# One row-tile pair for the lone rows of wo, other column groups for the last tile, and a new order of all work

## The chip, the cores and the metric

The kernel runs on one NeuronCore of a Trainium2 chip. The metric is device time in microseconds (us), the median over several executions. The core has TensorE (PE; its weight loads are shown as PEld), VectorE (DVE), ScalarE (ACT), GpSimd (POOL), and SyncE (SP), which here only issues DMAs. Matmuls read on-chip memory and write eight accumulator banks of 512 float32 columns (banks 0 to 7); DVE and ACT empty them.

## What is computed

x is 2048 tokens of 448 features. Two branches work on its layernorm and are added to it: linear attention with softmax feature maps of q and k (16 heads of 28), and an MLP mixer with token shifts.

```python
def _A_ref(x, wqkv, w_phi, wo):
    qkv = (x @ wqkv).reshape(B, S, 3, H, Dh).transpose(2, 0, 3, 1, 4)
    q, k, v = qkv[0], qkv[1], qkv[2]
    pq = einsum("bhsd,hdf->bhsf", q, w_phi); pk = einsum("bhsd,hdf->bhsf", k, w_phi)
    phi_q = concat([softmax(pq), softmax(-pq)]); phi_k = concat([softmax(pk), softmax(-pk)])
    kv = einsum("bhsf,bhsd->bhfd", phi_k, v); z = einsum("bhsf->bhf", phi_k)
    num = einsum("bhqf,bhfd->bhqd", phi_q, kv)
    den = einsum("bhqf,bhf->bhq", phi_q, z)[..., None] + 1e-6
    return (num / den).transpose(0, 2, 1, 3).reshape(B, S, D) @ wo

def _B_ref(x, w1, w2, w3, w4):
    h = gelu(layernorm(x) @ w1)
    # the four quarters of h's features are shifted by 1, -1, 2, -2 tokens
    x1 = x + concat([g0, g1, g2, g3]) @ w2
    return x1 + gelu(layernorm(x1) @ w3) @ w4

xn = layernorm(x)
out = x + _A_ref(xn, ...) + _B_ref(xn, ...)
```

## The kernel before

**An order written by hand.** Every operation is first recorded (`Recorder`, lines 20 to 222), each engine's stream in the order of recording. `solve()` (76) works out who must wait for whom; an engine waits only for semaphores, so the recording order is the order on each engine's queue, SP's and POOL's among them, and what two engines do at one time follows from the waits. Lines 118 to 120 hold PE's own rule: a matmul on a bank waits for earlier PE work on that bank if that came from another row tile (`lo != tile[0]`). All matmuls are recorded at line 204, all transposes on PE at 208, ACT's activations at 212, DVE's and POOL's operations at 216, DMA transposes at 219 and plain DMAs at 222, so the profile's lines are these helpers' and the tiles' names tell steps apart (some share memory: oT and o_tok lie in xnT's region, xs and outb in vaug's, h3T in phik's, eq in hi's, wo in wv's).

**Row tiles.** 448 rows are cut into four overlapping pieces of 128 that begin at 0, 128, 192 and 320 (`START`, 448). Nearly all matmuls use 64 rows, one on the array's lower half (`LO`) and one on its upper half (`HI`) at the same time. Rows 192 to 256 stand in two pieces, so in piece 1 or piece 2 one half is left out: seven steps of 64 rows make 448.

**The stages.** (1) `spin` and `hold` matmuls on constants keep PE busy until data is there. (2) `chain` (573 to 637, called at 969) lays out the first layernorm, transposes of xn (`XT`: on PE; `XD`: by DMA), v (`ZV`), w1 (`ZW`, `ZH`, `ZR`), the folding of w_phi into the q and k weights (`FO`), shifts of h (`h_shift`, six DMAs) and the start of the first token pair (`HF`: p = 0 k, 1 w2, 2 q; second number: first or second half). `L` holds layernorm steps: m statistics, r the root on POOL, q the root on ACT, a the apply on DVE, p on POOL. (3) `play` (1055) holds the rest as a list of steps: for token pairs k and q projections with exponentials (`k0`, `k1`, `q0`, `q1`), `w0`/`w1_` (w2 and its addition on DVE), `kn` (sums of phi_k on DVE), `kx` (their product on POOL), `K` (phi_k times v), `lo`/`sc`/`A` (second layernorm: statistics on DVE, scaling on POOL, apply on POOL or, for tiles in `on_dve`, on DVE), `G` and `T` (DMA transposes of its result and of exp(q)), `kc`/`kb` (the finished kv), `a`/`b` (w3 and its gelu), `N` (numerators: 16 matmuls, six DVE and two POOL operations, then a DMA transpose o_T), `f, 1..4, p` (for two tiles w4 and wo summed in banks 4 and 5, then `fin_out` on DVE) and `S` (the store).

**The end.** Tiles 14 and 15 come alone, after the list, with 128-row matmuls: `fin_full(14)` does 14 steps of w4 and four of wo at 448 columns; `fin_split(15, 256)` does the same for columns 0 to 256 and then 256 to 448, each followed by its addition and its store. Since four full pieces of wo would count rows 192 to 256 twice, `num_tile` (807 to 811) sets 64 columns of o_tok to zero for these two tiles.

Of the kernel before, what the change touches and what calls it, by code (L numbers as in the profile page):

```python
# [1111 lines left out]
```

## Time and profile before

| | us |
|---|---|
| median of three executions | 173.25 |
| lowest and highest | 173.14, 176.32 |
| the profiled execution | 172.24 |
| its span, first to last instruction | 170.5 |
| granted TensorE clock | 1.00 |

| engine | busy us | share |
|---|---|---|
| PE | 166.2 | 97% |
| DVE | 108.4 | 64% |
| POOL | 92.2 | 54% |
| ACT | 83.9 | 49% |

Times in the profile count from the span's start. A matmul's busy time is longer than its share of the array, because matmuls are pipelined; the distance from one start to the next tells what it costs. In the windows of the profile, after the length come busy us and number of instructions of PE, PEld, DVE, ACT and POOL, then the granted clock, the DMA engines' share and GB/s. In a timeline a bracket gives the idle time ahead of a group and who ended it.

### The profile page before, as it was taken

How to read it: one execution, taken by the hardware profiler on the slowest of the kernel's cores; microseconds unless marked ns; L12 is line 12 of the kernel's file. 1: busy time of each engine (PE TensorE's matmuls, PEld its weight loads, DVE VectorE, ACT ScalarE, POOL GpSimd, SP SyncE). 2: the span in 40 equal slices, each digit the busy share in tenths (PEclk: the TensorE clock that was granted, in tenths of full speed). 3: DMA queues.
4: the chain of work that ended last, by engine and by line, in shares of the span. 5: the costliest groups of instructions: out<-in, count | busy, mean ns of one | idle time of the engine just before them, and what ended most of it. 6: DMA issues, size and time to landing. Idle time of an engine off the chain costs nothing.

```text
span 170.5 us, 5420 instructions
## 1 busy us (share of the span) xinstructions
PE 166.2 (97%) x2351; PEld 96.3 (56%) x2351; DVE 108.4 (64%) x246; ACT 83.9 (49%) x114; POOL 92.2 (54%) x128
## 2 busy tenths in 40 slices
PE   8899999999999999999999999999999999999994
PEld 7576789655555555554554554554545555545463
DVE  3798865249999799967678933757407552425621
ACT  5789866879999879357242240421304222404000
POOL 6588590005799999992585272094420754023740
PEclk9999999999999999999999999999999999999999
DMA  5995677999599940569037949945440113021141
GB/s 153 359 207 99 150 84 210 190 351 171 118 134 191 257 98 0 142 126 94 0 64 136 113 96 168 139 105 78 92 115 0 35 31 112 4 58 31 31 117 48
DMA packets 51111, 20.07 MB, mean 118 GB/s; under 512 B 42256, under 2 KB 50384, under 8 KB 51088
## 3 DMA queue, kind: packets, MB, share of 16 engines
q1 hardware_dynamic: 49968, 18.86, 58.1%
q10 hardware_dynamic: 1120, 0.87, 1.5%
q8 instruction: 18, 0.29, 0.8%
q14 instruction: 5, 0.04, 0.1%
HBM read 7.14 MB, written 1.84 MB: 53 GB/s over the span
## 4 chain that ended last, share of the span: by engine, by line
PE 88%; DMA 5%; SPq 3%; DVE 1%; POOL 1%; issue 1%
PE banks L204 87%; SPq L222 3%; DMA hRT<-gT 2%; DMA xtok<-in_A_x_dram 2%; PE banks L208 1%; DVE st L216 1%; POOL rs L216 0%; POOL xn L216 0%; DVE xnT L216 0%; DVE mv L216 0%; DVE vaug L216 0%
## 5 line engine op out<-in xcount | busy, mean ns | idle before, releaser
L212 ACT ACTIVATE phik<-banks 128x1024 bf16<-128x1024 f32 (+1 forms) x44 | 41.8, 985 | 61.1 <-PE banks L204 61.0
L204 PE MATMUL banks<-gT,w 64*128 64x512 bf16 x392 | 48.0, 376 | 0.0
L216 DVE TENSOR_TENSOR vaug<-banks,vaug 128x464 f32<-128x464 f32 (+3 forms) x65 | 32.7, 513 | 23.1 <-PE banks L204 21.4
L204 PE MATMUL banks<-w,phik 64*128 64x448 bf16 (+3 forms) x434 | 45.2, 343 | 0.0
L216 POOL TENSOR_TENSOR xnT<-vaug 128x280 bf16<-128x280 f32 (+1 forms) x32 | 18.1, 586 | 45.9 <-DVE vaug L216 45.9
L204 PEld LDWEIGHTS banks<-w,phik 64*128 64x128 bf16 (+1 forms) x434 | 22.8, 94 | 19.1 <-issue 0.4
L204 PE MATMUL banks<-wv,xnT 64*128 64x448 bf16 (+3 forms) x222 | 32.4, 346 | 0.2
L734 POOL TENSOR_TENSOR phik<-phik,rks 128x1792 bf16<-128x1792 bf16 x8 | 25.6, 3212 | 9.1 <-DVE rks L216 8.8
L204 PEld LDWEIGHTS banks<-gT,w 64*128 64x128 bf16 x392 | 18.0, 94 | 18.4 <-ACT phik L212 0.7
L204 PEld LDWEIGHTS banks<-wv,xnT 64*128 64x128 bf16 (+1 forms) x222 | 14.0, 94 | 8.1 <-ACT xnT L212 0.8
L216 POOL TENSOR_TENSOR vaug<-xn,xtok 128x448 f32<-128x448 bf16 x16 | 16.2, 1031 | 1.1 <-DVE vaug L216 1.1
L216 DVE TENSOR_REDUCE ksum<-phik 128x64 f32<-128x1792 bf16 x8 | 16.0, 1996 | 0.2 <-ACT phik L212 0.2
L204 PE MATMUL banks<-xnT,w 64*128 64x512 bf16 (+1 forms) x105 | 16.0, 334 | 0.0
L212 ACT ACTIVATE hi<-banks 128x896 bf16<-128x896 f32 x16 | 13.7, 919 | 2.3 <-PE banks L204 2.3
L204 PE MATMUL banks<-wpk,xnT 64*128 64x448 bf16 x112 | 14.2, 349 | 0.0
L204 PE MATMUL banks<-wpq,xnT 64*128 64x448 bf16 x112 | 13.7, 349 | 0.0
L216 DVE RECIPROCAL vaug<-banks 128x16 f32<-128x16 f32 x16 | 4.1, 254 | 15.2 <-PE banks L204 15.2
L216 POOL TENSOR_TENSOR rs<-mv,mhalf 128x1 f32<-128x1 f32 (+1 forms) x15 | 10.4, 697 | 5.3 <-DVE mv L216 5.2
L204 PE MATMUL banks<-w,hT 64*128 64x448 bf16 x96 | 12.8, 349 | 0.0
L216 DVE TENSOR_TENSOR xn<-banks,xn 128x512 bf16<-128x512 f32 (+1 forms) x16 | 9.0, 601 | 3.6 <-PE banks L204 3.6
L216 DVE BATCH_NORM_STATS2 st<-xn 128x6 f32<-128x448 bf16 x16 | 9.4, 590 | 0.0
L216 DVE BATCH_NORM_STATS2 st<-xtok 128x6 f32<-128x448 bf16 x15 | 9.0, 601 | 0.4 <-DMA xtok<-in_A_x_dram 0.4
(71 smaller groups left out, 167.2 us busy)
## 6 DMA issues: line engine op xcount, KB each, us to landing
w<-in_B_w_dram SPq DMA_DIRECT2D x2, 896.0 KB, 5.7
out_dram<-vaug SPq DMA_DIRECT2D x15, 112.0 KB, 1.9
w<-in_B_w_dram SPq DMA_DIRECT2D x1, 1568.0 KB, 9.3
xtok<-in_A_x_dram SPq DMA_DIRECT2D x2, 448.0 KB, 6.3
wv<-in_A_wo_dram SPq DMA_DIRECT2D x2, 224.0 KB, 3.8
xtok<-in_A_x_dram SPq DMA_DIRECT2D x3, 112.0 KB, 3.9
xtok<-in_A_x_dram ACTq DMA_DIRECT2D x3, 112.0 KB, 4.1
w<-in_B_w_dram SPq DMA_DIRECT2D x1, 336.0 KB, 4.4
```

What stands on the lines that cost most here:

```text
L204: self.op("PE", lambda e: e.matmul(out, lhsT, rhs, start=start, stop=stop, skip_group_check=True), [out], [lhsT, rhs], tile=self._tile(lhsT))
L208: self.op("PE", lambda e: e.transpose(out, in_, ident), [out], [in_, ident], tile=self._tile(in_))
L212: self.op("ACT", lambda e: e.activation(out, in_, func, **kw), [out], [in_] + aps)
L216: self.op(eng, lambda e: getattr(e, name)(out, *args, **kw), [out], aps)
L222: self.op(eng, lambda e: e.dma_start(out, in_), [out], [in_], dma=True)
L734: R.op(pool, lambda e: e.tensor_tensor(ph, ph, wide, op=ALU.mult), [ph], [ph, wide, *after])
```

## The change

The two memsets go, and with them the double rows: `fin_full(14)` now takes pieces 0, 2 and 3 of wo, `fin_split(15)` pieces 0, 1 and 3. The 64 rows that are left out (128 to 192 for tile 14, 256 to 320 for tile 15) are done ahead of both, by `fin_tails`, as one pair of 64-row matmuls: tile 14 on the lower half into bank 0, tile 15 on the upper half into banks 1 and 3. They start those banks' sums, and PE's rule in `solve()` now also waits where the size of the row tiles has changed. The last tile's column groups become 320 and 128 (256 and 192 before). Bank numbers, the set of tiles that DVE normalizes, and the order in both lists are new; the play list has the same steps as before. In the chain, tile 8 goes through PE instead of a DMA transpose, `v_out` of tiles 8 to 11 goes from ACT to DVE, and the two numbers at the chain's end (the lag that the layout gives the upper half, and how many jobs from the end it stops alternating the shares of the halves) go from 500, 2 to 300, 0. In the play list N(15) stands ahead of f(3, 5) instead of ahead of f(3, 6). Below, the lists are cut.

```diff
@@ -116,7 +116,7 @@
                     mode = (tile[1], mode[1] + 1)
                 for k in w:
                     for lo, (i, m) in tiles.setdefault(k, {}).items():
-                        if lo != tile[0]:
+                        if lo != tile[0] or m != mode[1]:
                             need["PE"] = max(need.get("PE", -1), i)
                     tiles[k][tile[0]] = (pos["PE"], mode[1])
             kn = known[eng]
@@ -806,9 +806,6 @@
-            if i >= NT - 2:
-                c0 = 192 + 64 * (i % 2)
-                R.ew(pool, "memset", o_tok[:, i % 4, c0:c0 + 64], 0.0)
@@ -832,24 +829,30 @@
         def fin_bank(i):
             return (0 if i > 13 else 4) + i % 2
 
+        def fin_tails(i, cut):
+            x_sum(i)
+            g, j = divmod(i, 4)
+            c = 128 * j
+            R.mm(banks[0][:, 0:D], oT[0:64, g % 2, 1, c:c + 128], wo[0:64, 1, :], True, False)
+            for n, (c0, c1) in enumerate(((0, cut), (cut, D))):
+                R.mm(banks[2 * n + 1][:, c0:c1], oT[64:128, g % 2, 2, c + 128:c + 256], wo[64:128, 2, c0:c1], True, False)
+
+        def fin_steps(b, i, c, kcs):
+            g, j = divmod(i, 4)
+            s = slice(128 * j, 128 * j + 128)
+            for fc in range(FC):
+                R.mm(b[:, c], h3T[:, g % 2, fc, s], w4[:, fc, c], False, False)
+            for kc in kcs:
+                R.mm(b[:, c], oT[:, g % 2, kc, s], wo[:, kc, c], False, kc == KC - 1)
+
         def fin_full(i):
-            g, j = divmod(i, 4)
-            b = banks[fin_bank(i)]
-            x_sum(i)
-            for fc in range(FC):
-                R.mm(b[:, 0:D], h3T[:, g % 2, fc, 128 * j:128 * j + 128], w4[:, fc, :], fc == 0, False)
-            for kc in range(KC):
-                R.mm(b[:, 0:D], oT[:, g % 2, kc, 128 * j:128 * j + 128], wo[:, kc, :], False, kc == KC - 1)
+            fin_steps(banks[0], i, slice(0, D), (0, 2, 3))
 
         def fin_split(i, cut):
-            g, j = divmod(i, 4)
             x_sum(i)
             for n, (c0, c1) in enumerate(((0, cut), (cut, D))):
                 b, c = banks[2 * n + 1], slice(c0, c1)
-                for fc in range(FC):
-                    R.mm(b[:, c], h3T[:, g % 2, fc, 128 * j:128 * j + 128], w4[:, fc, c], fc == 0, False)
-                for kc in range(KC):
-                    R.mm(b[:, c], oT[:, g % 2, kc, 128 * j:128 * j + 128], wo[:, kc, c], False, kc == KC - 1)
+                fin_steps(b, i, c, (0, 1, 3))
                 R.ew(dve, "tensor_tensor", outb[:, i % 4, c], b[:, c], xs[:, i % 2, c], op=ALU.add)
                 R.dma(out2d[128 * i:128 * i + 128, c], outb[:, i % 4, c], "SP" if n else "ACT")
 
-        fb = {(1, 0): 3, (1, 2): 1, (0, 0): 3, (0, 2): 1}
+        fb = {(1, 0): 3, (1, 2): 1, (0, 0): 4, (0, 2): 1}
-        kq = {0: (2, 3), 1: (1, 3), 2: (0, 1), 3: (0, 3), 4: (1, 0), 5: (1, 2), 6: (1, 2), 7: (1, 0)}
-        wb = {0: 0, 2: 2, 4: 2, 6: 2, 8: 0, 10: 0, 12: 2, 14: 2}
+        kq = {0: (2, 3), 1: (1, 3), 2: (0, 1), 3: (2, 3), 4: (1, 0), 5: (1, 2), 6: (1, 2), 7: (1, 0)}
+        wb = {0: 0, 2: 2, 4: 0, 6: 2, 8: 0, 10: 0, 12: 2, 14: 2}
-        vb = {0: 2, 1: 5, 2: 4, 3: 6, 4: 5, 5: 4, 6: 6, 7: 7, 8: 0, 9: 7, 10: 1, 11: 4, 12: 7, 13: 0, 14: 5, 15: 3}
-        gb = ((7, 2, 3), (1, 7, 0), (1, 0, 3), (4, 5, 6))
+        vb = {0: 7, 1: 0, 2: 1, 3: 6, 4: 5, 5: 4, 6: 1, 7: 4, 8: 0, 9: 3, 10: 2, 11: 1, 12: 7, 13: 0, 14: 3, 15: 5}
+        gb = ((7, 2, 3), (1, 0, 5), (0, 7, 6), (7, 5, 6))
...
-            HD(3, 3), HD(3, 3), do(load_wT, 0, (1, 2, 3)), L(("m", 0)), HD(6, 3), L(("r", 0, 1), ("a", 0), ("v", 1)),
-            HD(2, 3), L(("m", 2), ("q", 1, 1), ("m", 3)), XT(0, 2, 1, "ACT"),
-            L(("p", 1), ("q", 2, 1), ("a", 2), ("r", 3, 1), ("m", 5), ("m", 4), ("p", 3)), HD(4, 3), HD(5, 3),
-            inside(3, ZV(0, EV(0, "ACT", 1)), XT(1, 5, 1, "ACT")), XT(2, 0, 1, "ACT"), ZV(1, EV(1, "ACT", 1)),
-            L(("q", 5, 1)), inside(1, ZV(2, EV(2, "ACT", 1)), XT(3, 0, 1, "ACT")),
-            L(("m", 6), ("q", 6, 1), ("p", 5), ("q", 4, 1), ("m", 7)), ZH(2, 0), L(("a", 6), ("a", 4)),
...
-            L(("r", 10, 1)), XD(8), L(("p", 10), ("m", 9), ("r", 11, 1)), XD(10), ZV(14, EV(14, "ACT", 1)), do(phi_blocks),
-            ZV(13, EV(13, "ACT", 1)), L(("a", 11)), XD(11), L(("r", 9, 1)), FO(1, 2, 0), do(load_w3, 0),
-            inside(2, ZW(3, 2, EW(3, 2, 1)), FO(1, 2, 1)), inside(2, ZV(12, EV(12, "ACT", 1)), FO(1, 0, 0)), FO(1, 0, 1),
-            do(h_shift, 0), ZW(3, 1, EW(3, 1, 1)), inside(1, ZV(8, EV(8, "ACT", 1)), FO(0, 2, 0)), L(("p", 9)),
-            XT(9, 3, 1, "DVE"), FO(0, 2, 1), ZR(0, 6, (rest_out, 0, 6), (rest_T, 0)), ZV(9, EV(9, "ACT", 1)), do(late_3),
-            FO(0, 0, 0), ZV(10, EV(10, "ACT", 1)), inside(1, ZR(1, 2, (rest_out, 1, 2)), FO(0, 0, 1)), ZW(2, 1, EW(2, 1, 1)),
-            ZV(11, EV(11, "ACT", 1)), ZW(2, 2, EW(2, 2, 1)), ZW(2, 0, EW(2, 0, 1)), HF(2, 0), HF(0, 0), do(load_w4),
-            do(kv_picks), do(h_shift, 1), HF(1, 0), do(kv_ones), do(rest_T, 1), HF(0, 1), HF(1, 1), HF(2, 1)], 500, 2)
-
-        on_dve = (7, 8, 12, 13, 15)
+            HD(5, 3), HD(6, 3), L(("m", 0), ("r", 0, 1)), HD(1, 3), L(("a", 0), ("v", 1), ("q", 1, 1)), XT(0, 6, 1, "ACT"),
+            L(("m", 2)), HD(0, 3), L(("m", 3), ("q", 2, 1), ("a", 2), ("m", 5), ("q", 3, 1), ("m", 4), ("p", 1)), HD(3, 3),
+            L(("m", 7)), HD(2, 3), inside(2, ZV(0, EV(0, "ACT", 1)), XT(1, 0, 1, "ACT")), XT(2, 3, 1, "ACT"),
+            ZV(1, EV(1, "ACT", 1)), L(("q", 5, 1), ("p", 3), ("p", 5)),
+            inside(1, ZV(2, EV(2, "ACT", 1)), XT(3, 3, 1, "ACT")), L(("q", 4, 1), ("m", 6)), ZH(1, 0), L(("q", 7, 1)),
+            do(load_wT, 0, (1, 2, 3)), L(("p", 4)), inside(1, ZH(0, 0), XT(5, 5, 1, "ACT")), ZH(0, 1, EW(0, 0, 1)),
...
+            L(("a", 10)), XD(10), L(("r", 11, 1), ("r", 8, 1), ("m", 9), ("a", 11), ("a", 8)), do(phi_blocks), XD(11),
+            L(("r", 9, 1)), do(late_3), ZV(13, EV(13, "ACT", 1)), do(load_w3, 0), XT(8, 3, 1, "DVE"), FO(1, 2, 0),
+            inside(2, ZW(3, 2, EW(3, 2, 1)), FO(1, 2, 1)), inside(2, ZW(3, 1, EW(3, 1, 1)), FO(1, 0, 0)), FO(1, 0, 1),
+            inside(2, ZV(12, EV(12, "ACT", 1)), FO(0, 2, 0)), ZV(8, EV(8, "DVE", 1)), L(("p", 9)), XT(9, 3, 1, "2"),
+            do(h_shift, 0), FO(0, 2, 1), ZR(0, 6, (rest_out, 0, 6), (rest_T, 0)), FO(0, 0, 0), ZV(9, EV(9, "DVE", 1)),
+            ZV(11, EV(11, "DVE", 1)), ZV(10, EV(10, "DVE", 1)), FO(0, 0, 1), ZW(2, 1, EW(2, 1, 1)), do(load_w4),
+            ZW(2, 2, EW(2, 2, 1)), ZW(2, 0, EW(2, 0, 1)), HF(0, 0), ZR(1, 1, (rest_out, 1, 1)), HF(2, 0), HF(0, 1),
+            do(h_shift, 1), HF(1, 0), HF(2, 1), HF(1, 1), do(kv_picks), do(kv_ones), do(rest_T, 1)], 300, 0)
+
+        on_dve = (5, 11, 13, 15)
...
-            (k0, 1), (kn, 0), (w0, 2), (k1, 1), (k0, 2), (T, 0), (kx, 0), (lo, 1), (w1_, 2), (kn, 1), (k1, 2), (q0, 1),
-            (q0, 2), (q1, 1), (kn, 2), (q1, 2), (w0, 4), (k0, 3), (w1_, 4), (T, 1), (k1, 3), (kx, 1), (q0, 3), (k0, 4),
...
-            (k1, 6), (K, 2), (q0, 6), (kn, 5), (w0, 10), (q1, 6), (w1_, 10), (G, 2), (lo, 7), (kx, 4), (lo, 5), (lo, 4),
-            (G, 0), (k0, 7), (lo, 6), (K, 7), (kn, 6), (kx, 5), (K, 6), (k1, 7), (q0, 7), (w0, 12), (q1, 7), (w1_, 12),
-            (sc, 4), (a, 0), (A, 6), (A, 4), (kx, 6), (G, 6), (kn, 7), (K, 1), (K, 10), (b, 0), (a, 1), (K, 9), (lo, 10),
-            (K, 11), (wo_in,), (K, 8), (b, 1), (w0, 14), (G, 4), (a, 2), (a, 3), (b, 2), (b, 3), (A, 7), (lo, 11), (A, 5),
-            (lo, 8), (kx, 7), (w1_, 14), (G, 5), (K, 13), (a, 4), (G, 7), (T, 12), (lo, 9), (a, 5), (b, 4), (K, 12), (T, 14),
...
-            (f, 1, 3), (a, 20), (S, 4), (f, 2, 3), (a, 19), (f, 3, 3), (b, 19), (f, 4, 3), (b, 20), (N, 10), (a, 21),
-            (f, 1, 4), (b, 21), (N, 11), (f, 2, 4), (N, 13), (a, 22), (f, 3, 4), (b, 22), (a, 23), (f, 4, 4), (a, 24),
-            (b, 23), (f, 1, 5), (a, 25), (S, 7), (b, 24), (S, 9), (b, 25), (S, 6), (N, 12), (f, 2, 5), (a, 27), (S, 8),
-            (f, 3, 5), (a, 26), (f, 4, 5), (S, 10), (N, 14), (b, 27), (b, 26), (f, 1, 6), (f, 2, 6), (N, 15), (f, 3, 6),
-            (S, 11), (S, 12), (S, 13)])
+            (k0, 1), (w0, 2), (k1, 1), (k0, 2), (kn, 0), (kx, 0), (w1_, 2), (k1, 2), (q0, 1), (q0, 2), (q1, 1), (T, 0),
+            (k0, 3), (q1, 2), (lo, 0), (k1, 3), (kn, 1), (w0, 4), (kn, 2), (q0, 3), (w1_, 4), (k0, 4), (T, 1), (T, 3),
...
+            (q1, 6), (A, 2), (T, 6), (A, 1), (kn, 5), (G, 3), (G, 2), (w1_, 10), (kx, 4), (lo, 7), (G, 1), (G, 0), (lo, 6),
+            (K, 5), (lo, 4), (kx, 5), (k0, 7), (K, 6), (lo, 5), (K, 7), (k1, 7), (q0, 7), (w0, 12), (q1, 7), (w1_, 12),
+            (sc, 4), (A, 7), (a, 0), (K, 11), (K, 9), (A, 4), (kn, 6), (K, 8), (A, 6), (a, 1), (A, 5), (b, 0), (kx, 6),
+            (b, 1), (G, 7), (w0, 14), (kn, 7), (lo, 8), (a, 2), (K, 10), (a, 3), (b, 2), (b, 3), (lo, 10), (kx, 7), (lo, 11),
+            (G, 5), (wo_in,), (lo, 9), (w1_, 14), (K, 12), (a, 4), (a, 5), (b, 4), (G, 6), (K, 13), (G, 4), (K, 14), (K, 15),
+            (sc, 8), (b, 5), (a, 6), (kc,), (kb,), (b, 6), (A, 8), (T, 11), (A, 9), (G, 8), (A, 11), (a, 7), (N, 1), (b, 7),
...
+            (G, 13), (N, 9), (a, 18), (f, 3, 2), (a, 17), (f, 4, 2), (N, 8), (b, 17), (b, 18), (f, 1, 3), (N, 11), (G, 15),
+            (f, 2, 3), (N, 10), (a, 19), (f, 3, 3), (S, 4), (a, 20), (S, 5), (f, 4, 3), (b, 20), (b, 19), (N, 13), (f, 1, 4),
+            (a, 22), (T, 15), (a, 21), (S, 7), (N, 12), (f, 2, 4), (b, 21), (b, 22), (f, 3, 4), (a, 23), (f, 4, 4), (a, 24),
+            (N, 14), (b, 23), (S, 6), (f, 1, 5), (b, 24), (f, 2, 5), (a, 25), (N, 15), (f, 3, 5), (b, 25), (a, 26),
+            (f, 4, 5), (a, 27), (b, 26), (b, 27), (S, 10), (f, 1, 6), (S, 11), (S, 9), (S, 8), (f, 2, 6), (f, 3, 6), (S, 13),
+            (S, 12)])
+        fin_tails(14, 320)
         fin_full(14)
-        fin_split(15, 256)
+        fin_split(15, 320)
```

More of the change, by code (lines that the diff above doesn't have):

```diff
@@ L980, in bass_parallel_sum__linear_kernel_hedgehog__mixer_s_mlp__prompt_kernel @@
-            L(("r", 15, 1)), XT(12, 4, 1, "ACT"), ZV(6, EV(6, "ACT", 1)), L(("a", 14), ("a", 15), ("a", 13)), do(load_w2),
-            XT(14, 2, 2, "2"), inside(2, ZW(1, 0, EW(1, 0, 1)), XT(13, 4, 1, "DVE")), L(("r", 8, 1), ("p", 8)),
-            ZV(7, EV(7, "ACT", 1)), L(("m", 10)), ZW(3, 0, EW(3, 0, 1)), L(("m", 11)), ZV(15, EV(15, "ACT", 1)),
-            L(("r", 10, 1)), XD(8), L(("p", 10), ("m", 9), ("r", 11, 1)), XD(10), ZV(14, EV(14, "ACT", 1)), do(phi_blocks),
-            ZV(13, EV(13, "ACT", 1)), L(("a", 11)), XD(11), L(("r", 9, 1)), FO(1, 2, 0), do(load_w3, 0),
@@ new lines, in bass_parallel_sum__linear_kernel_hedgehog__mixer_s_mlp__prompt_kernel @@
+            ZV(1, EV(1, "ACT", 1)), L(("q", 5, 1), ("p", 3), ("p", 5)),
+            inside(1, ZV(2, EV(2, "ACT", 1)), XT(3, 3, 1, "ACT")), L(("q", 4, 1), ("m", 6)), ZH(1, 0), L(("q", 7, 1)),
+            do(load_wT, 0, (1, 2, 3)), L(("p", 4)), inside(1, ZH(0, 0), XT(5, 5, 1, "ACT")), ZH(0, 1, EW(0, 0, 1)),
+            L(("a", 7)), ZH(2, 0), L(("m", 14), ("r", 14, 1), ("q", 6, 1)), inside(2, ZH(2, 1), XT(4, 4, 1, "ACT")),
+            XT(7, 0, 1, "DVE"), ZV(3, EV(3, "ACT", 1)), L(("a", 6)), ZV(5, EV(5, "ACT", 1)), do(load_w2), L(("m", 15)),
@@ new lines, in bass_parallel_sum__linear_kernel_hedgehog__mixer_s_mlp__prompt_kernel @@
+            XT(6, 0, 1, "DVE"), ZV(4, EV(4, "ACT", 1)), ZH(1, 1, EW(0, 1, 2)), ZW(1, 0, EW(1, 0, 1)),
+            L(("m", 12), ("p", 14), ("r", 15, 1), ("r", 12, 1), ("m", 13), ("p", 15)), ZW(1, 1, EW(1, 1, 1)),
+            ZW(1, 2, EW(1, 2, 1)), L(("m", 8), ("a", 12), ("m", 10)), XT(14, 2, 2, "DVE"), XT(12, 6, 1, "ACT"),
+            L(("r", 13, 1)), ZV(7, EV(7, "ACT", 1)), L(("p", 13)), ZV(6, EV(6, "ACT", 1)), XT(13, 6, 1, "ACT"),
+            ZV(14, EV(14, "ACT", 1)), ZV(15, EV(15, "ACT", 1)), L(("m", 11), ("r", 10, 1)), ZW(3, 0, EW(3, 0, 1)),
@@ new lines, in bass_parallel_sum__linear_kernel_hedgehog__mixer_s_mlp__prompt_kernel @@
+            (q1, 3), (kx, 1), (kn, 3), (k1, 4), (w0, 6), (q0, 4), (w1_, 6), (K, 0), (q1, 4), (kx, 2), (lo, 1), (K, 2),
+            (K, 4), (lo, 3), (k0, 5), (K, 1), (lo, 2), (T, 2), (T, 4), (k1, 5), (q0, 5), (kx, 3), (w0, 8), (sc, 0), (q1, 5),
+            (kn, 4), (T, 7), (k0, 6), (w1_, 8), (T, 5), (A, 3), (k1, 6), (A, 0), (K, 3), (q0, 6), (load_w3, 1), (w0, 10),
+            (q1, 6), (A, 2), (T, 6), (A, 1), (kn, 5), (G, 3), (G, 2), (w1_, 10), (kx, 4), (lo, 7), (G, 1), (G, 0), (lo, 6),
+            (K, 5), (lo, 4), (kx, 5), (k0, 7), (K, 6), (lo, 5), (K, 7), (k1, 7), (q0, 7), (w0, 12), (q1, 7), (w1_, 12),
```

19 lines of the change are left out of this document (5 added, 14 removed).

## The prediction

> **What bounds the kernel now.** I read the page first. Its shares of busy time and its chain of waits say the same thing.
>
> ```profile
> PE 166.2 (97%) x2351; PEld 96.3 (56%) x2351; DVE 108.4 (64%) x246; ACT 83.9 (49%) x114; POOL 92.2 (54%) x128
> ...
> PE 88%; DMA 5%; SPq 3%; DVE 1%; POOL 1%; issue 1%
> ```
>
> The reader is to see that TensorE (PE) leaves only 4.3 us of the 170.5 us span. To find them I asked for the busy time by stretches (window, length, then PE, PEld, DVE, ACT, POOL).
>
> ```profile
> 0.00:8.00 8.00, 6.66 (x98) 5.41 (x100) 4.15 (x12) 4.64 (x11) 4.57 (x24) 1.00 0.79 248
> 8.00:12.00 4.00, 3.72 (x75) 2.40 (x73) 3.83 (x13) 3.48 (x10) 3.17 (x7) 1.00 1.58 264
> ...
> 32.00:36.00 4.00, 3.73 (x39) 2.47 (x38) 1.00 (x8) 2.68 (x5) 0.31 (x1) 1.00 1.06 228
> ...
> 60.00:70.00 10.00, 10.00 (x200) 5.76 (x198) 9.79 (x17) 8.12 (x9) 9.62 (x7) 1.00 0.30 59
> 161.00:170.50 9.50, 7.07 (x56) 4.96 (x54) 2.56 (x5) 0.00 (x0) 2.61 (x4) 1.00 0.26 74
> ```
>
> PE is idle at the start (1.3 + 0.3), once at 32 to 36 (0.3) and after its last matmul (2.4). Elsewhere it is full, but around 60 to 70 DVE and POOL are nearly full too: there a re-ordering can do harm. The chain in order of time names the idle spot at 34.
>
> ```profile
> 25.39 0.43 DVE xnT L216
> ...
> 30.29 3.90 DMA hRT<-gT
> 34.19 0.05 issue
> 34.24 133.85 PE banks L204 x1759
> 168.11 0.36 DVE vaug L216
> ```
>
> Between 25.87 and 30.25 this chain has seven issues on SP's queue of about 0.6 us each (load_w3, then the six copies of h_shift(0)); behind them comes rest_T(0), and the first w2 half of tile 0 waits for it. From 34.24 all is PE, to the end. Last, the timeline of the end:
>
> ```profile
> 161.04 2.82 PE L204 MATMUL banks<-w,phik 128*128 128x448 bf16 x14
> 163.70 0.92 PE L204 MATMUL banks<-wv,xnT 128*128 128x448 bf16 x4
> 164.46 1.69 PE L204 MATMUL banks<-w,phik 128*128 128x256 bf16 x14
> 165.99 0.60 PE L204 MATMUL banks<-wv,xnT 128*128 128x256 bf16 x4
> 166.43 1.32 PE L204 MATMUL banks<-w,phik 128*128 128x192 bf16 x14
> 167.58 0.49 PE L204 MATMUL banks<-wv,xnT 128*128 128x192 bf16 x4
> 168.11 0.36 DVE L216 TENSOR_TENSOR vaug<-banks,vaug 128x192 bf16<-128x192 f32 x1 [1.06 <-PE banks L204]
> ```
>
> **The last two tiles.** From start to start, 14 matmuls take 2.66 us at 448 columns (190 ns each), 1.53 at 256 (109) and 1.15 at 192 (82): columns / 2.4 GHz plus 2 to 3 ns. The change takes one full-height wo step from each tile: 190 + (109 + 82) = 381 ns off. The row-tile pair adds 190 ns: its lower half has 448 columns, its upper half 320 and 128, side by side. The solver's new clause adds a wait: the first 128-row matmul on bank 0 waits for the lower half to end. In the trace a 64x448 matmul takes 349 ns, and the last pair of before (160.76) is followed by a 128-row matmul at 161.04, 0.28 us later instead of 0.19. With the wait it is 0.349 plus about 0.06 (a 64x128 pair ahead of such a wait: 216 ns of matmul, 279 to the next start), 0.41. So the tails cost 0.19 + 0.13 against 0.38: -0.06 us; if the wait is free, -0.19. I take -0.1. Queued behind that wait are only the last 51 matmuls.
>
> [...]
>
> The last group shrinks from 192 to 128 columns. Its matmuls are not in the trace at this shape: by the slope 56 ns, and no worse than the 82 ns of 192 columns, so between 0 and 17 x 26 ns = +0.45 us. The slope fits three shapes; I take 0 (the sum of columns is unchanged). The last DVE add falls from 0.36 by 0.06 (256 columns: 0.42) and the last store from 48 KB to 32 KB; stores of 64 and 48 KB land in 1.6 and 1.5 us, so -0.1. The first group's add (0.42 at 256, 0.62 at 448: about 0.5) and its store end before the last one, since 0.95 us of matmuls follow that group. Tail in all: -0.25 us. The two memsets (0.15 us each on POOL) sit beside PE work: nothing. The tails need o_T(15) some 5 us earlier than before; in the new list N(15) stands 12 us of PE work ahead of them, against some 6.5 us from its matmuls to its landing (157.7 to 161.67 plus the median 2.4 here).
>
> **The start (chain up to HF).** One tile less goes through DMA transposes (XD 8, about 1.6 us on SP's queue) and four v_out copies of 0.54 us go from ACT to DVE, which has 3.0 us idle in 28 to 32. h_shift(0) now stands ahead of ZR(0) and starts some 1.6 us earlier, so rest_T(0) goes out when rest_out(0) is done (about 28.7) instead of at 30.29, and its data lands 1.5 us earlier. Moreover HF(1,0), which waited, now has HF(0,1) and ZR(1) ahead of it. The wait goes: PE's record has a gap from 33.62 + 0.19 to 34.24, 0.43 us, and PEld 0.7; I take -0.5 (bounds 0 and -0.7). What is late next is k_exp(0): HF(0,1) ahead of HF(1,0) brings it forward. The waits for tiles 2 and 3 (0.32 and 0.23 us idle): tile 3 gets its root from ACT (0.20) instead of POOL (0.63), but that root now stands ahead of tile 1's eviction on ACT and waits for statistics ready at 7.2 us, so tile 1, evicted at 7.08 before, goes about 0.35 later. Between -0.5 and +0.4; I take -0.1. Tile 8 through PE adds four pairs of 29 ns: +0.1.
>
> **The middle (play list).** PE's own order is almost unchanged; what moves is the DVE, POOL and SP work. Up to kx(7) POOL has the same work before and after: eight products of 3.21, two scalings of 1.2, seven applies of 0.77 us. It runs without a stop from 44.56 to 75.34 but for 0.8 us. kn(6), 2.5 us on DVE, goes behind w1_12: in DVE's queue it now starts at 66.4 instead of 64.88 and ends at 68.9. POOL, with three applies instead of two ahead of kx(6), comes there at 68.7. So kx(6) runs 69.0 to 72.2 (before 67.92 to 71.12), while its first reader K(12) comes at about 73.4; kx(7) ends at 75.4 against 75.34. Each N, with its 16 matmuls, six DVE and two POOL operations and its transpose on SP's queue, stands at least 10 us of PE work ahead of its attention step, and needs 6.5. N(15)'s DVE operations (157.92 to 160.23, 2.3 us) now stand ahead of fin_out(10) and (11), which free banks 4 and 5 for the last up-projections; 2.8 us of PE work lie between, so DVE is free just in time. S(8) to S(11) go behind o_T(15) on SP's queue, and fin_out(12) and (13) write their buffers: transpose 1.2, four issues of 0.6 and a landing of 1.9 after N(15)'s POOL work end 2 us before fin_out(12) is due. Price 0, with +0.1 for chance misses. Cover lost: if DVE falls over 0.8 us behind, PE pays all that is beyond it.
>
> **Sum.** -0.25 - 0.5 - 0.1 + 0.1 + 0.1 = -0.65 us, against the profiled execution's 172.24 us (span 170.5 and 1.74 around it): 171.6. The three runs have a median of 173.25, 1.0 above it, so I forecast 172.6.
>
> **The rivals.** *DVE's queue takes over (slower).* For it: DVE's only idle times from 38 to 76.9 are 0.20, 0.84, 0.18 and 1.36 us, and kn(0), kn(1), kn(6) and kn(7) go 2 to 5 us of PE work later in the list. If two kn (2.5 us each) come late, kx(6), kx(7), the K steps and kv_blocks follow, and PE with them: 5.0 less 0.8 of cover is +4.2 us, with the gains 176.8; one late gives +1.7, 174.3. It decides once kx(7) ends later than 76.2. Against it: the count above. Chance of any of this 0.2, of beyond 2% 0.12.
>
> *The wait at 34 only changes its name* (rest_out(1) or the fold copies, which compete with four more copies on DVE). Then the -0.5 is gone: 173.1. Chance 0.2.
>
> *The last group is set by its weight loads.* The 14 loads at 192 columns were busy 1.20 us, 86 ns each. If they can't hide behind a 56 ns matmul, 17 x 30 ns = +0.5 us: 173.1. For it: nothing here shows a 128-row load behind a short matmul. Against it: 64-row loads show 94 ns and still start in pairs every 29 ns (transposes). Chance 0.1. [...]
>
> *Much faster.* It takes 3.5 us. The idle spots hold 1.9 us before the tail, and the tail's store stays: chance 0.04.
>
> **Numbers.** Forecast 172.6 with chance 0.46; the two small rivals (0.3 together) lie within half a us of it. Its own terms run from -0.35 - 0.7 - 0.5 + 0.1 (171.8) to 0.25 + 0 + 0.4 + 0.1 + 0.1 (174.1). With the scatter between executions (172.24 to 173.25 here) and one late kn, the range is 171.2 to 174.5. A measurement of this kernel can tell about 2% from no change, 3.5 us: faster 0.04, within 0.84, slower 0.12.
>
> **What would show it.** The chain of waits should hold no hRT landing ahead of the long PE piece; the last stretch should have 17 matmuls of each shape, the 128-column ones every 56 ns, and one 64-row pair ahead; the first 128-row matmul should start about 0.41 us after that pair. kx(7) should end before K(14) is due, with DVE's idle times in 50 to 75 smaller, not gone. I am wrong if PE shows gaps between 45 and 80 that end on POOL phik or DVE xn, or if the start loses more than half a us.

## The result and the profile after

Over 14 executions each on one chip, the changed kernel has a median of 171.96 us (171.55 to 174.16), the kernel before 173.52 (171.81 to 176.32). The ratio is 0.9927 [0.9902, 0.9952]: 1.3 us faster, within 2%. It leaves out executions that lie over 1.5% above the fastest of their kernel; the medians and the ranges here hold all of them. The forecast was 172.6, in a range of 171.2 to 174.5.

The two profiled executions are much closer than the medians: 172.24 us with a span of 170.5 before, 171.86 with 170.1 after. After, the profile is an ordinary execution; before, it was a good one. So there are two questions: where the 0.4 us of the profiles come from, and where another 1 us of the medians does.

The page's busy times, its chain by engine, and the busy time by stretches (window, length, then PE, PEld, DVE, ACT, POOL, granted clock, DMA share, GB/s) after:

```profile
PE 166.4 (98%) x2359; PEld 95.0 (56%) x2359; DVE 110.8 (65%) x249; ACT 81.7 (48%) x112; POOL 91.3 (54%) x125
...
PE 95%; DMA 1%; DVE 1%; POOL 0%; issue 0%; DVEq 0%
```

```profile
0.00:8.00 8.00, 6.77 (x96) 5.04 (x98) 4.25 (x13) 4.72 (x12) 4.38 (x25) 1.00 0.79 245
8.00:12.00 4.00, 4.00 (x80) 3.03 (x80) 3.37 (x9) 3.61 (x11) 2.41 (x5) 1.00 1.76 269
...
32.00:36.00 4.00, 4.00 (x74) 2.67 (x70) 1.00 (x8) 3.14 (x4) 0.31 (x1) 1.00 0.88 255
60.00:70.00 10.00, 9.95 (x184) 5.73 (x182) 9.36 (x17) 7.94 (x9) 9.60 (x8) 1.00 0.27 54
161.00:170.10 9.10, 6.74 (x54) 4.28 (x51) 2.51 (x5) 0.00 (x0) 2.02 (x2) 1.00 0.16 50
```

PE's idle spots at 8 to 12 and at 32 to 36 are gone from this profile, and the chain holds PE alone from 25 us to the last addition, with no landing of hRT:

```profile
25.19 39.53 PE banks L204 x605
64.73 0.05 issue
64.78 92.69 PE banks L204 x1250
157.47 0.05 issue
157.51 3.62 PE banks L204 x36
161.15 6.66 PE banks L204 x51
167.81 0.02 issue
167.84 0.29 DVE vaug L216
```

Busy time hides how much a full PE does. So I also counted the work: each matmul's columns at 2.4 GHz, the slope of the distances from start to start before (190 ns at 448 columns, 109 at 256, 82 at 192), and half of it for a 64-row matmul: in the fence below, 14 pairs of 64x448 take 2.66 us from start to start (157.51 to 160.17), as do 14 single matmuls of 128x448 (161.15 to 163.81). The work is 157.9 us in both kernels; span less work is what is lost. Lost up to a given time, in us (a step is about 0.2):

| lost by | 12 us | 28 us | 32 us | 36 us | 40 us | 72 us | 160 us | end |
|---|---|---|---|---|---|---|---|---|
| before | 5.35 | 6.25 | 6.24 | 6.95 | 7.12 | 7.93 | 9.70 | 12.55 |
| after | 5.00 | 5.77 | 5.92 | 6.00 | 6.45 | 7.40 | 9.22 | 12.26 |

In the profiles 0.35 us come by 12 us, and by 36 us it is 0.95, most of it the wait for hRT (0.71 lost in 32 to 36 before, 0.08 after). By 40 us only 0.67 is left, because PE now waits at 36.99, where w2's second half waits for ACT's exponentials (the bracket gives the idle time of the weight loads ahead of it):

```profile
36.99 0.30 PEld L204 LDWEIGHTS banks<-w,hT 64*128 64x128 bf16 x6 [0.43 <-ACT phik L212]
```

More is lost again later: the chain is cut at 64.78, where w3's first step stands right behind the landing of a transposed second layernorm tile (64.69), and at 157.51. The last tiles after, by shape:

```profile
157.51 2.82 PE L204 MATMUL banks<-w,phik 64*128 64x448 bf16 x28
160.17 0.92 PE L204 MATMUL banks<-wv,xnT 64*128 64x448 bf16 x9
161.15 2.82 PE L204 MATMUL banks<-w,phik 128*128 128x448 bf16 x14
163.81 0.73 PE L204 MATMUL banks<-wv,xnT 128*128 128x448 bf16 x3
164.38 2.06 PE L204 MATMUL banks<-w,phik 128*128 128x320 bf16 x14
166.28 0.57 PE L204 MATMUL banks<-wv,xnT 128*128 128x320 bf16 x3
166.69 0.94 PE L204 MATMUL banks<-w,phik 128*128 128x128 bf16 x14
167.47 0.33 PE L204 MATMUL banks<-wv,xnT 128*128 128x128 bf16 x3
167.84 0.29 DVE L216 TENSOR_TENSOR vaug<-banks,vaug 128x128 bf16<-128x128 f32 x1 [0.46 <-PE banks L204]
```

Fourteen matmuls of 320 columns take 1.90 us from start to start (136 ns each), fourteen of 128 columns 0.78 (56 ns each): the slope of columns / 2.4 GHz holds at both new shapes.

### The profile page after: what moved, and what is told of

Read it like the earlier page. It is cut to its first block, busy times and chain, and to the rows that moved or that the text cites. A ratio compares the mean times of both kernels' runs of the same rounds, so it can differ in the third digit from the quotient of the medians.

```text
span 170.1 us, 5438 instructions
## 1 busy us (share of the span) xinstructions
PE 166.4 (98%) x2359; PEld 95.0 (56%) x2359; DVE 110.8 (65%) x249; ACT 81.7 (48%) x112; POOL 91.3 (54%) x125
## 4 chain that ended last, share of the span: by engine, by line
PE 95%; DMA 1%; DVE 1%; POOL 0%; issue 0%; DVEq 0%
PE banks L204 94%; PE banks L208 1%; DMA xtok<-in_A_x_dram 1%; DVE st L216 0%; POOL rs L216 0%; DVE xn L216 0%; DVE vaug L216 0%; DVE mv L216 0%; DVEq L166 0%
## 5 line engine op out<-in xcount | busy, mean ns | idle before, releaser
L204 PEld LDWEIGHTS banks<-w,phik 64*128 64x128 bf16 (+1 forms) x434 | 22.3, 94 | 20.1 <-PE banks L204 0.8
L204 PE MATMUL banks<-wv,xnT 64*128 64x448 bf16 (+3 forms) x222 | 31.5, 346 | 0.0
L204 PEld LDWEIGHTS banks<-gT,w 64*128 64x128 bf16 x392 | 18.6, 94 | 18.3 <-ACT phik L212 1.0
L204 PEld LDWEIGHTS banks<-wv,xnT 64*128 64x128 bf16 (+1 forms) x222 | 13.5, 94 | 7.9 <-ACT xnT L212 0.5
L204 PE MATMUL banks<-wpk,xnT 64*128 64x448 bf16 x112 | 14.9, 349 | 0.0
L204 PE MATMUL banks<-wpq,xnT 64*128 64x448 bf16 x112 | 14.2, 349 | 0.0
L204 PE MATMUL banks<-w,hT 64*128 64x448 bf16 x96 | 12.6, 349 | 0.0
L216 POOL TENSOR_TENSOR rs<-mv,mhalf 128x1 f32<-128x1 f32 (+1 forms) x13 | 9.3, 731 | 2.7 <-DVE mv L216 2.7
L216 POOL TENSOR_SCALAR g_tok<-xn,rs 128x512 bf16<-128x512 bf16 x12 | 9.1, 767 | 0.8 <-DMA gT<-g_tok 0.5
```

The costliest lines, as they stand in the source:

```text
L204: self.op("PE", lambda e: e.matmul(out, lhsT, rhs, start=start, stop=stop, skip_group_check=True), [out], [lhsT, rhs], tile=self._tile(lhsT))
L216: self.op(eng, lambda e: getattr(e, name)(out, *args, **kw), [out], aps)
```

## The experiments

No kernel here leaves out any part of the computation. Each ratio is against the kernel before, measured beside the run; its medians there were 173.82, 173.75 and 173.46 us.

### Which part of the change carries the gain

**before_again**: the kernel before, unchanged, measured once more.

> The kernel before once more, for a second profile. Its executions so far lie between 171.8 and 175.7 us, the profiled one at 172.24 us. Theory D: the scatter sits in the wait for the landing of hRT near 34 us, so a slower execution shows a longer gap of PE there (0.43 us in the first profile, over 1 us in an execution above 173.2 us), and elsewhere the same. Theory E: the scatter is spread over the start (arrival of the x tiles, 0 to 12 us), and the gap at 34 stays near 0.4 us.

172.32 us, span 170.6. PE waits again for hRT at 34.30 (0.50 us), and lost by 36 us is again 6.95. The wait is part of this kernel, and both profiles of it show one of its good executions. So this profile could not tell what makes an execution slow.

**head_only**: the kernel before with the new chain, and **rest_only**: the changed kernel with the old chain.

```diff
 head_only, against before
-        fb = {(1, 0): 3, (1, 2): 1, (0, 0): 3, (0, 2): 1}
+        fb = {(1, 0): 3, (1, 2): 1, (0, 0): 4, (0, 2): 1}
...
-            do(kv_picks), do(h_shift, 1), HF(1, 0), do(kv_ones), do(rest_T, 1), HF(0, 1), HF(1, 1), HF(2, 1)], 500, 2)
+            do(h_shift, 1), HF(1, 0), HF(2, 1), HF(1, 1), do(kv_picks), do(kv_ones), do(rest_T, 1)], 300, 0)
```

> The kernel before with only the new chain of the start (job list, bank tables vb, gb and fb, and the numbers 300 and 0); play list and end as before. Theory H, the gain is made in the start, where PE has lost 0.95 us less by 36 us, and is kept: ratio 0.994 to 0.996, and no hRT landing in the chain of waits. Rival M, what PE gains in the start is taken back between 36 and 75 us, where DVE, ACT and POOL are nearly full: 0.998 to 1.000, with new gaps there. Theory D (scatter of the kernel before comes from the hRT wait): these runs spread over less than 1 us, as those of the changed kernel mostly do.

> The changed kernel with the chain of the start as before: new play list, bank pairs, tails and column groups. Theory H: 0.998 to 1.000, the tail's 0.25 us less the new gap of 0.23 us at 157 us, and PE's gap at 34 us is there again. Rival M: 0.993 to 0.996, the play list and the end hold the gain. Theory D: these runs spread over 2 us or more, as those of the kernel before.

head_only: 172.13 us, ratio 0.9919 [0.9886, 0.9952], all of the gain. rest_only: 174.43 us, ratio 1.0058 [1.0015, 1.0100]; without the new chain, the new play list and the new end gain nothing. But rest_only's profile does not show the wait at 34 first. Its chain shows this:

```profile
21.37 5.11 DMA xnT<-xn
26.48 0.14 issue
26.62 1.55 PE banks L204 x12
```

That is XD(8), the DMA transpose of tile 8, which the old chain has and the new one does not. Its landing comes 5.11 us after its issue, and PE waits 2.0 us for it, from 24.6 to 26.6. In the profile of before it was the first of three and landed soonest, after 2.5 us:

```profile
L219 SPq DMA_TRANSPOSE xnT<-xn x3: 1259/1277/2183, 21.0 to 23.6; - x3
...
DMA to landing us min/median/max: 2.5/3.4/4.1
...
24.16 0.35 PE L204 MATMUL banks<-wv,xnT 64*128 64x448 bf16 x1
```

It was issued at 21.02 and landed at 23.55, and ZV(8) starts at 24.16: 0.6 us to spare, so that no wait in that profile names it. rest_only's profile is of an execution with the clock at 0.99, the slowest of its twelve; the nine at full clock, at 172.8 to 175.2 us, have no profile.

### The wait for hRT, and a wait that was not on the list

**hf_swap**: the kernel before, with k's second half of tile 0 ahead of w2's first half, so that PE has other work while hRT lands.

```diff
-            do(kv_picks), do(h_shift, 1), HF(1, 0), do(kv_ones), do(rest_T, 1), HF(0, 1), HF(1, 1), HF(2, 1)], 500, 2)
+            do(kv_picks), do(h_shift, 1), HF(0, 1), HF(1, 0), do(kv_ones), do(rest_T, 1), HF(1, 1), HF(2, 1)], 500, 2)
```

> The kernel before with one job moved: HF(0, 1), the second half of the first k pair, stands ahead of HF(1, 0), the w2 half that waits for hRT. Theory H: 0.65 us of matmuls now cover the wait, PE's gap of 0.43 us at 34 us is gone and the ratio is 0.997 to 0.998 (-0.4 us; k_exp comes earlier too). Rival M: the gap goes and PE waits instead for ACT or DVE between 36 and 40 us, ratio 0.999 to 1.001. Theory D: the spread of the runs shrinks as well.

175.69 us, ratio 1.013 [1.006, 1.020]: all six executions took over 174.4 us, though the order is that of before up to 30 us. The wait at 34 is gone from the trace, but 0.88 us are lost between 36 and 40 (0.17 in before), at stops at 38.1 and 39.9, so in this profile the wait moved and nothing was saved there. A larger loss stands ahead of it. The chain:

```profile
22.15 4.41 DMA xnT<-xn
26.55 0.14 issue
26.69 1.00 PE banks L204 x12
```

and the page's slices of PE's busy time and granted clock, 4.4 us each:

```profile
PE   8799968999999999999999999999999999999994
PEclk9999996999999999999999999999999999999999
```

PE idles 1.87 us for tile 8, and in the slice behind that the clock drops. The stretches of this run say how far (the clock is the third number from the end):

```profile
24.00:28.00 4.00, 2.13 (x43) 1.58 (x38) 1.15 (x2) 1.29 (x3) 2.39 (x3) 0.96 0.84 96
28.00:32.00 4.00, 4.00 (x98) 3.70 (x94) 1.36 (x2) 1.38 (x3) 0.00 (x0) 0.61 0.89 286
```

The trace's clock record has half speed from 27.70 to 31.12: 3.41 us, and full speed again after. By 28 us 8.73 us are lost, by 32 us 10.31; in before 6.25 and 6.24. So the wait costs some 2 us and the half clock 1.6 more. The same stands in rest_only (half speed 26.93 to 30.35; 9.04 lost by 28 us, 10.28 by 32). A new theory follows: the kernel before has a wait for tile 8 whose length changes from execution to execution, with a stretch at half clock behind it where it is long (1.87 and 2.0 us in these two profiles), and the changed kernel is rid of both because tile 8 goes through PE.

**xt8**: the kernel before with tile 8 through PE, its other order kept.

```diff
-            L(("r", 10, 1)), XD(8), L(("p", 10), ("m", 9), ("r", 11, 1)), XD(10), ZV(14, EV(14, "ACT", 1)), do(phi_blocks),
-            ZV(13, EV(13, "ACT", 1)), L(("a", 11)), XD(11), L(("r", 9, 1)), FO(1, 2, 0), do(load_w3, 0),
+            L(("r", 10, 1)), L(("p", 10), ("m", 9), ("r", 11, 1)), XD(10), ZV(14, EV(14, "ACT", 1)), do(phi_blocks),
+            ZV(13, EV(13, "ACT", 1)), L(("a", 11)), XD(11), L(("r", 9, 1)), XT(8, 3, 1, "DVE"), FO(1, 2, 0), do(load_w3, 0),
```

> The kernel before with one job replaced: tile 8 of xn is transposed by PE (XT, evicted by DVE) instead of by a DMA transpose (XD). Two profiles of the last call showed PE waiting 1.9 and 2.0 us for that DMA's landing near 26.6 us, and the TensorE clock at half for 3.41 us right behind it. Theory W: this wait, with the half-clock window that follows it, is what most executions of the kernel before pay; ratio 0.990 to 0.994, spread of the runs below 1 us but for single ones, clock 1.0. Theory H (the landing of hRT at 34 us is what counts, the DMA of tile 8 is an accident): ratio 0.997 to 1.000 and a spread as before.

172.80 us (172.32 to 173.86), ratio 0.9955 [0.9925, 0.9984], between what the two theories expected. None of the 12 executions lies above 173.9, and all have the full clock; of the 22 beside it five were granted 0.99, at 173.5 to 176.5. In its profile the wait for hRT is gone as well (0.19 us lost in 32 to 36). Its transpose was issued as late as in before (30.37 against 30.29), but landed after 2.96 us instead of 3.90; why is not known. Against that it has a cost of its own, in the chain:

```profile
21.82 0.60 ACT hT L212
22.42 0.52 ACT vaug L212
22.94 0.05 issue
22.99 0.31 PE banks L208 x8
```

PE waits half a us for an eviction on ACT, to have bank 3 for the transposes; in the changed kernel's profile the transposes of tile 8 start at 21.11 without a wait. The start of this profile was also slow (6.09 lost by 12 us), where the order is still that of before.

**w2_later**: the kernel before, the load of w2 moved behind XD(11), so that the transposes are issued ahead of it.

```diff
-            L(("r", 15, 1)), XT(12, 4, 1, "ACT"), ZV(6, EV(6, "ACT", 1)), L(("a", 14), ("a", 15), ("a", 13)), do(load_w2),
+            L(("r", 15, 1)), XT(12, 4, 1, "ACT"), ZV(6, EV(6, "ACT", 1)), L(("a", 14), ("a", 15), ("a", 13)),
...
-            ZV(13, EV(13, "ACT", 1)), L(("a", 11)), XD(11), L(("r", 9, 1)), FO(1, 2, 0), do(load_w3, 0),
+            ZV(13, EV(13, "ACT", 1)), L(("a", 11)), XD(11), do(load_w2), L(("r", 9, 1)), FO(1, 2, 0), do(load_w3, 0),
```

> The kernel before with load_w2 (three DMAs, 2.7 us of issues on SP's queue) moved behind the DMA transposes of tiles 8, 10 and 11. Tile 8's transpose then goes out near 18.5 us instead of 21 and lands by 23.5; h_shift(0) and rest_T(0) keep their place, so PE's wait for hRT at 34 us stays (0.3 to 0.5 us). Theory W: ratio 0.991 to 0.996, clock 1.0, narrow spread, with the gap at 34 us still there. Theory H: no change, 0.999 to 1.002.

173.64 us, ratio 0.9999 [0.9966, 1.0031]: no change, where the theory of tile 8 had expected 0.991 to 0.996. XD(8) was issued at 18.55 and landed at 23.4, after 4.9 us: earlier issue, longer landing, and 0.5 us ahead of its reader (23.99) in this profile. Two of 12 executions still came at 176.5 with the clock at 0.99. PE's longest wait in this profile is for hRT:

```profile
PE banks L204 <- DMA hRT<-gT: 0.9, 1, 0.9
```

Its transpose was issued at 30.29, as in before, and landed after 4.29 us instead of 3.90. So the move of w2 is not what gives the gain. Whether the load of w2, now behind the transposes, made hRT's landing longer is not shown.

**after_xd8**: the changed kernel, tile 8 by DMA again.

```diff
-            L(("a", 10)), XD(10), L(("r", 11, 1), ("r", 8, 1), ("m", 9), ("a", 11), ("a", 8)), do(phi_blocks), XD(11),
-            L(("r", 9, 1)), do(late_3), ZV(13, EV(13, "ACT", 1)), do(load_w3, 0), XT(8, 3, 1, "DVE"), FO(1, 2, 0),
+            L(("a", 10)), XD(10), L(("r", 11, 1), ("r", 8, 1), ("m", 9), ("a", 11), ("a", 8)), do(phi_blocks), XD(8), XD(11),
+            L(("r", 9, 1)), do(late_3), ZV(13, EV(13, "ACT", 1)), do(load_w3, 0), FO(1, 2, 0),
```

> The changed kernel with tile 8 by DMA transpose again, issued between those of tiles 10 and 11. Theory W: PE waits 1 to 3 us for its landing near 25 us, the clock falls to half in many executions, and the changed kernel's gain is gone: ratio 0.999 to 1.010, wide spread. Theory H: the gain stays, 0.992 to 0.995.

175.51 us (174.51 to 176.84), ratio 1.0123 [1.0062, 1.0183]: this one edit takes back the gain of the whole change and more. Here XD(8) stands behind XD(10), so this is not before's own order; it is issued at 22.27 and lands after 4.89 us. PE's timeline, the first halves of v:

```profile
24.11 0.35 PE L204 MATMUL banks<-wv,xnT 64*128 64x448 bf16 x1
...
27.29 0.35 PE L204 MATMUL banks<-wv,xnT 64*128 64x448 bf16 x1 [2.83 <-DMA xnT<-xn]
...
28.39 0.55 PE L204 MATMUL banks<-wv,xnT 64*128 64x448 bf16 x1
28.74 0.58 PE L204 MATMUL banks<-wv,xnT 64*128 64x448 bf16 x1
29.11 0.58 PE L204 MATMUL banks<-wv,xnT 64*128 64x448 bf16 x1
```

The bracket is the idle time and who ended it. Behind it a 64x448 matmul takes 0.58 us instead of 0.35, and the next starts 0.36 later instead of 0.19: half speed, from 28.40 to 31.81 by the clock record, 3.41 us once more.

**xd8_filled**: the same, with 45 pairs of `hold` matmuls on constants ahead of ZV(8). They add nothing to the result; they keep PE busy during the wait.

```diff
-            inside(2, ZV(12, EV(12, "ACT", 1)), FO(0, 2, 0)), ZV(8, EV(8, "DVE", 1)), L(("p", 9)), XT(9, 3, 1, "2"),
+            inside(2, ZV(12, EV(12, "ACT", 1)), FO(0, 2, 0)), HD(3, 45), ZV(8, EV(8, "DVE", 1)), L(("p", 9)), XT(9, 3, 1, "2"),
```

> after_xd8 (changed kernel, tile 8 by DMA transpose) with 45 pairs of matmuls on constants (64x128, 2.5 us) ahead of tile 8's v matmuls. They add nothing to the result and stand where PE waited 2.83 us for the landing. [...]

175.19 us (174.68 to 175.60), ratio 1.0112 [1.0077, 1.0146]. The author's estimate, if the half clock comes from the wait, was the full clock and 173 to 174.3 us: the clock held, the time was longer. The wait became work:

```profile
25.31 2.82 PE L204 MATMUL banks<-const-bfloat16-1.0 64*128 64x128 bf16 x90 [0.47 <-DVE wpk L216]
27.97 0.35 PE L204 MATMUL banks<-wv,xnT 64*128 64x448 bf16 x1
```

and behind it the 64x448 matmuls keep 0.35 us; no slice of this profile is below full speed. All six executions have the full clock. after_xd8 had it in three of six: those took 174.51, 174.58 and 175.22 us, and the three with a mean clock of 0.99 took 175.81, 176.53 and 176.84. So with the wait filled the half clock did not come (none of six executions against three of six, which is few; 1.6 us lie between the means of the two groups of three). The wait itself stays, now spent on filler: the mean of the six, 175.19, lies 0.4 us above that of after_xd8's full-clock executions. In the profile tile 8 had landed at 27.54, so the filler ran 0.4 us too long. What is left against the changed kernel, about 3 us, is mostly the wait for tile 8: 2.4 us of the profile's 3.6 are the filler's work, and 0.7 were lost by 12 us, ahead of any of it.

### The end

Beside these stands **after_again**, the changed kernel once more.

> The changed kernel once more, as the base for the next two and for tails_between: median 171.8 to 172.2 us.

171.89 us (171.50 to 174.12), ratio 0.9919 [0.9891, 0.9947]: the result repeats. Its profile (171.82 us) is not rid of the wait for hRT: the transpose was issued at 28.49 and landed at 34.13, after 5.64 us (29.01, 32.89 and 3.88 in the first profile), the first step with hRT stands 0.39 us behind the one before it instead of 0.19, and 0.51 us are lost from 32 to 36.

**old_tail**: the changed kernel with the end of before (two memsets, four steps of wo, groups of 256 and 192). **cut_256**: the changed kernel with the column groups of before only.

```diff
 old_tail, against the changed kernel
+            if i >= NT - 2:
+                c0 = 192 + 64 * (i % 2)
+                R.ew(pool, "memset", o_tok[:, i % 4, c0:c0 + 64], 0.0)
...
-        fin_tails(14, 320)
         fin_full(14)
...
-        fin_split(15, 320)
+        fin_split(15, 256)
```

> The changed kernel with the old end: two memsets, four full pieces of wo for tiles 14 and 15, groups 256 and 192, no fin_tails. From the two profiles: 381 ns of matmuls more, the pair's 190 ns and its wait of 125 ns less, the last addition 70 ns and the last store about 60 ns longer. If the terms add up, 0.15 to 0.25 us slower than after_again; if the end gives nothing because of the new waits, within 0.05 us of it.

> The changed kernel with the last tile's groups at 256 and 192 columns, tails kept. The same matmul columns; the last addition 0.36 instead of 0.29 us and the last store 48 instead of 32 KB. 0.07 to 0.15 us slower than after_again; rival (narrow matmuls bound by their weight loads): up to 0.4 us faster.

old_tail: 171.94 us, ratio 0.9931 [0.9906, 0.9957]. cut_256: 172.36 us, ratio 0.9962 [0.9928, 0.9995]. Both intervals overlap after_again's, so no time here tells the ends apart: old_tail's median is 0.05 us above after_again's where 0.15 to 0.25 was expected, and cut_256's is 0.47 above where 0.07 to 0.15 was expected, though its end lies between the other two. The traces can be compared from the start of f(3, 6) to the span's end. In old_tail these are

```profile
157.38 2.82 PE L204 MATMUL banks<-w,phik 64*128 64x448 bf16 x28
160.03 0.73 PE L204 MATMUL banks<-wv,xnT 64*128 64x448 bf16 x6
```

and an end at 170.2, so 12.8 us; 12.6 in the changed kernel (157.51 to 170.1), 12.7 in cut_256 (157.58 to 170.3). One profile each: 0.1 for the pair of tails and 0.1 for the groups, about as the sum had them (0.1 and 0.15).

**tails_between**: the changed kernel with the pair of tails between f(2, 6) and f(3, 6), because these two now stand side by side and the trace showed a stop of 0.41 us between their starts (157.10 to 157.51) instead of 0.19.

```diff
-            (f, 4, 5), (a, 27), (b, 26), (b, 27), (S, 10), (f, 1, 6), (S, 11), (S, 9), (S, 8), (f, 2, 6), (f, 3, 6), (S, 13),
+            (f, 4, 5), (a, 27), (b, 26), (b, 27), (S, 10), (f, 1, 6), (S, 11), (S, 9), (S, 8), (f, 2, 6), (fin_tails, 14, 320), (f, 3, 6), (S, 13),
...
-        fin_tails(14, 320)
+        x_sum(14)
```

> The changed kernel with fin_tails recorded between f(2, 6) and f(3, 6), so that the row-tile pair fills PE's wait for its own earlier half-tile matmuls (228 ns beyond the normal distance at 157.5 us of the changed kernel's profile) and the first 128-row matmul no longer waits for the pair (125 ns). If these two waits are set by PE's own order: the end is 0.3 to 0.4 us earlier, ratio 0.990 to 0.993. Rival: the switch of the row tiles costs the same wherever it stands, 0.992 to 0.994 and the gaps only move.

171.77 us (171.37 to 171.89), ratio 0.9898 [0.9865, 0.9930]: the best of all versions here, though its distance to the changed kernel's 171.96 and 171.89 is within their scatter. Its trace shows why it may be real:

```profile
157.80 2.82 PE L204 MATMUL banks<-w,phik 64*128 64x448 bf16 x28
160.46 0.73 PE L204 MATMUL banks<-wv,xnT 64*128 64x448 bf16 x6
161.12 0.36 PE L204 MATMUL banks<-w,phik 128*128 128x448 bf16 x1
```

From the last start of f(2, 6) to the first 128-row matmul, with the pair inside in both, it needs 3.74 us (157.38 to 161.12), the changed kernel 4.05 (157.10 to 161.15). The pair covers the stop before f(3, 6), and the first 128-row matmul starts 0.28 us behind the last pair of f(3, 6) instead of 0.41.

## Why the prediction held, and where it did not

**The wait for hRT (-0.5): right, but part of it came back 3 us later.** The work lost in 32 to 36 us went from 0.71 (0.80 in before_again) to 0.08 (0.08 to 0.14 in head_only, old_tail, cut_256 and tails_between, but 0.51 in after_again): -0.65, within the bounds. The transpose was issued 1.3 us earlier and landed 1.3 us earlier, about as forecast (28.7 and 1.5). Its rival, that the wait only changes its name, came in part, and by another name than the two listed: at 37 PE waits for ACT's exponentials. From 32 to 40 us 0.88 is lost before (1.16 in before_again) and 0.53 after (0.38 to 0.68 in the other five with tile 8 on PE and the new start), so -0.35 in the two profiles.

**Tiles 2 and 3 (-0.1): right in sign, perhaps too small.** Lost by 12 us: 5.15 to 6.09 in six profiles with the old chain (before, before_again, w2_later, rest_only, hf_swap, xt8), 4.85 to 5.67 in eight with the new one. The means are 5.51 and 5.14: -0.4, near the low bound of -0.5 to +0.4, but the two groups overlap. Which of the edits did it was not tried.

**Tile 8 through PE (+0.1): the step that failed, by its size.** The prediction counted four pairs of transposes on PE and 1.6 us on SP's queue, and asked of the removed XD(8) only who stood behind it. It did not ask when its data lands and who waits for that, since in the profile shown nobody did. It lands 2.5 to 5.1 us after its issue; issued at 21.0, as in the profile of before, and needed at 24.16, that is between 0.6 us early and 2 us late. The profile's own slowest transpose of that kind, 4.07 us for tile 10, would have put it 0.9 us late. hf_swap, rest_only and after_xd8 show 1.9 to 2.8 us of waiting in their profiles; xt8, with that edit alone, takes the median of before down by 1 us, though not all of that is tile 8 (hRT goes too, and bank 3 comes in).

**The 1.0 us to the median: the same error in another place.** The sum gave 171.6 for the profiled execution (-0.65), against 171.86 measured (-0.38). Then 1.0 was added, as if the distance from the profiled execution to the median belonged to the chip. It belonged to the kernel before: the 69 executions of it beside all these runs spread over 171.6 to 174.9 at full clock (52 of them) and 173.5 to 176.5 at 0.99 (17), while the changed kernel's profiled 171.86 lies close to its medians (171.96 and 171.89), and 24 of its 26 executions are at full clock (171.5 to 173.1). That the whole of before's spread at full clock comes from tile 8, hRT and the start together is argued, not shown: no profile fell on one of its executions near 173.5. So the median of 171.96 lies inside the range, but not by the forecast's road: it had the same 0.65 us for the profiles and the medians, and 0.4 and 1.6 came.

**The tail (-0.25): right in its terms, given back by one it lacked.** From the first 128-row matmul to the end of the last addition: 7.43 us before (161.04 to 168.47), 6.98 after (161.15 to 168.13): -0.45, where the steps off and the shorter addition made -0.44. The pair and the first 128-row matmul are 0.41 us apart, as forecast, so the wait was not free. From the last addition's end to the span's end, with the last store, it is 1.97 us instead of 2.03. The rival that weight loads set the last group is out: 56 ns a matmul, not the 86 of its loads (the 14 loads of w4's steps in this group were busy 0.90 us, 64 ns each). The prediction saw that N(15) moves, but not that this leaves f(2, 6) and f(3, 6) side by side, each half of the array taking over the bank that the other had just written: +0.22 us, in all seven profiles with the new list as it is (after, after_again, old_tail, cut_256, rest_only, after_xd8, xd8_filled), and gone in tails_between.

**The middle (0): right on DVE's queue, with a small loss that it did not have.** No stop ends on POOL's phik or on DVE's xn between 45 and 80 us, and kx(7) ended at 74.9 (75.4 forecast, 76.2 the bound), so the rival of DVE's queue did not come. From 40 to 72 us 0.95 is lost, 0.81 before; the stop at 64.78 (0.40 us from start to start instead of 0.19) is more than that difference. It stands in four of six profiles with the new start and with tile 8 on PE: in after, after_again, tails_between and in head_only, which has the old list; not in old_tail and cut_256. A like stop of 0.5 us stands at 69.2 in rest_only and at 69.8 in after_xd8, and none in the five profiles with the old list and the old chain or one edit of it. So the list alone is not its cause, and it was followed no further.

## What to carry to other kernels

A DMA with 0.6 us to spare in one good profile can be on the critical path of other executions, as rest_only and hf_swap show (waits of 2.0 and 1.9 us) with the same order up to there: for every transfer that a change moves or removes, set its landing against the time of its first reader, with the longest landing of its kind in the trace and not the one that happened. Before adding the distance between a profiled execution and the median to a forecast, ask whether what scatters is something that the change removes. And when steps move out of a list, look at which neighbours they leave side by side.
